# A gated Fourier mixer and state-space layer on one core: the scan over odd tokens only, products with W summed on VectorE, and turned x copied by VectorE

## The chip, the cores and the metric

One core of one Trainium2 chip runs the whole kernel. The metric is the device time of one execution in microseconds. A time is the median of several executions. Durations of single instructions come from one profiled execution, whose span runs from its first to its last instruction.

## What is computed

The input x has 2048 tokens of 1024 channels in bf16. Two branches work on the same x, and a gate per token mixes them (cut to what matters):

```
g = sigmoid((x * gate_w).sum(-1, keepdims=True))

# branch A: Fourier mixing over tokens and channels
X = rfft2(x);  X = X * (w_r + 1j * w_i);  a = irfft2(X)

# branch B: a diagonal complex recurrence over the tokens
Lam_bar = exp(exp(log_dt) * Lam)
Bu = einsum("bld,pd->blp", x, B_bar)
for t in range(L):
    h = Lam_bar * h + Bu[:, t, :]
b = 2.0 * einsum("blp,dp->bld", hseq, Cmat).real + x * Dskip

out = g * a + (1 - g) * b
```

The recurrence is the part with a serial nature: 2048 steps, 1024 complex states. Both Fourier transforms are done as matrix products in stages.

## The kernel before

The kernel writes its order by hand. The string `ORDER` holds one letter per step; each letter advances one generator (the table `acts`, from line 1167), and the letter v runs the next piece of the recurrence, in the order that `PIECES` gives. `SLOTS` says which of four PSUM slots (two banks each) the next PSUM tile takes. The order of the letters is thus the order of the instructions in each engine's queue: TensorE (PE in the profile), VectorE (DVE), ScalarE (ACT), GpSimd (POOL) and the queue of SyncE that issues most DMAs (SPq). An engine works through its own queue in order and waits where its next instruction's data or buffer is not ready.

The stages, with their letters:

- **Turning x** (x, T, U). x is loaded (`load_x`, L234), twelve of its sixteen column groups are transposed by TensorE into PSUM (`turn`, L913), and the other four by DMA. `turn_out` (L922) copies each of the sixteen groups into xQ, 1024 elements per partition: ScalarE does all of them. In xQ a chunk of 256 tokens lies in runs of eight tokens.
- **Forward Fourier transform** (f, F, E, S, A, 1). `fold` (L933) makes sums and differences on VectorE. `fd` (L420) is the transform over channels, `fd_out` (L446) copies its result out of PSUM, `s1` (L454) is the first part of the transform over tokens, `s1_out` (L466) copies that out. `FD_DVE` and `S1_DVE` name the copies that VectorE does (four and three of sixteen each); ScalarE does the others. `s1_store` (L478) writes to DRAM scratch. The gate is formed on the way (g, e).
- **Input product of branch B** (h, H). `unit_mm` (L391) is the product of x with B, 32 matmuls per step. It reads a whole chunk of xQ, and each turn step writes a sixteenth of every chunk, so all sixteen copies have to be done before the first h. `unit_out` (L402) casts the result to bf16 on ScalarE.
- **Recurrence** (v, `recur`, L334). There are eight chunks of 256 tokens; the first two are handled in two halves of four state blocks each, the others in one piece with eight blocks, so there are ten groups. States are rotated by tables (`make_tab`, L272, letter t) so that the step of the recurrence has a real factor, the radius r. A group is: two products with the tables (`cross`, `along`), a sum and a difference (`join_re`, `join_im`), the carry from the chunk before (`carry_in`), two scans (`scan`, L361; real and imaginary part, each over all tokens and blocks of the group), the carry to the next chunk (`carry_part`, `carry_sum`), two products back (`cross`, `along`), a sum and a difference (`out_re`, `out_im`). All of these run on VectorE.
- **Output product of branch B** (n, o). `c_half` (L707) and `c_part` (L722): sixteen matmuls of 512 columns for half of a tile of 128 tokens. They need the whole chunk's recurrence. Tiles 13 to 15 (`c_part`) end the kernel; tiles 14 and 15 need the last chunk.
- **Middle of the Fourier branch** (s, 3, 4, 5, 6, 7, 8). `s2` (L587) ends the transform over tokens, `s2_out` (L599) copies out, `times_w` (L612) multiplies with W on VectorE, `is1` (L621) is the first part of the inverse transform. A complex product has four real products; `times_w` forms the four and `is1` adds them up on TensorE: it takes four passes of eight matmuls for each of the eight groups, with four sign variants of its constant MT.
- **End of the Fourier branch** (i, I, l, p, z, P, Z, R, Q, D and others). `is2`, `spectral_mm`, `spectral_out`, and `spectral` (L820), sums and differences on VectorE; then the two branches are added and rows are stored (`close`, L856; `last_out`, L896; `last_store`, L903).

The lines of the scan in `recur`:

```
seg = u[:, ri, j:j + m].rearrange("p j t -> p (j t)")
nc.vector.tensor_tensor_scan(out=seg, data0=rz[...], data1=seg, initial=0.0, op0=ALU.mult, op1=ALU.add)
...
work.extend((lambda: scan(0, 0, n), lambda: scan(1, 0, n)))
```

Of the kernel before, what the change touches and what calls it, by code (L numbers as in the profile page):

```python
# [26 lines left out]
NCH = S // TC  # L27
NEARLY = 10
# [9 lines left out]
FD_DVE = (2, 4, 6, 7)  # L38
CAST_ACT = (5, 6, 7)
ANG_ACT = (4, 5, 6, 7)  # L40
CARRY_POOL = ()
S1_DVE = (1, 4, 5)
CLOSES = (0, 1, 2, 3, 10, 4, 5, 11, 12, 6, 7, 8, 9)
PIECES = (
# [6 lines left out]
)  # L51
SLOTS = (
    "0123012310231023102310230123012031201312031203101230132031231031201312303312013213021021013010320130",
    "1220123203201320130130120321023120320321021023120312301230231201302303120",
# [3 lines left out]
    "xxxTVUVVVaTfVVrrUGTGG|Tfaaa|UafFffftafftUftxFEfTETUFffU22xSEkSTSTArxAfffUAUFTTEUfffUFbxwxbxbbTUEFbfE",  # L58
    "1bT~SSUfuFSFAUUUU2bbtbfAF1AtbbtrFttrbEffE11EbEh11SStbttfttttAg1~HtfufhA~tetFSSFrKHrtu1EAvfAEhtttvttt",
    "SSFtbbvvvAtEttH1Avthtftv1cttwv1tcthccctttvtcch~HFtvftHvvhuHtvfStEettStAHhtAeKrvFctcvvFhEEHKtvwtcSvtS",  # L60
    "hvvKc1vcc1vAAKKvv1c1v1hcvswcsLMvvveHHekMYsssnNHvvhHnsvvvJWWMvs3vsvNvvsssssnvssnvvs4NMvv4Njvhv553vhvv",
    "YvyJJL46H4vv5WWvhh5vvvMM78Jj7HHmn3nHvv8M44m6MnN77WW5jv+Yy5vvv3M845+mNY8nMJJMyvvv+467hvHMh5vN7N34vHmh",
    "4J8m+6n3h8v77HmH+55v4n64JMvNnMYy5vW83n+v7N474vJ568vYmmNJ7dh7NWj+v58v5vyvvd88MhvHHm8+MJm6h+n378vv7Hh8",
    "J+d4Y4YX5vv5NnJH6XXv7ny7mNNm8+hn8hvqivvvvvJvqyHihYivvyiqhivqqiYvNImvni+qJJmHIIiini+HinvdIIH+vvIIIqIN",
    "IiiiNmI+vvIInvvImvyJqii%NJINIJYJYmhvvv+vvvlylzvhHmplpzZZH+mZZZhlZvhPPRR++zyRRRlQDQHzRZZmRHZ+ZRZvoOZD",
    "QvlpDzzPovOvQBvZZlpPYvZZvBZDZRDRRRvzQDoloOBzoQOopZOoPOBlzlZRoDDZZvBZZRpQvzCvYZZvZZBZZPRDoQoo9RQQ9yRR",
    "0RRyCooD099C9Y990DD0D0Y00",
# [6 lines left out]
HALF_PI = float(np.pi / 2)  # L74


def _host_consts():
# [15 lines left out]
    for u in range(4):  # L93
# [42 lines left out]
        MT=b16(np.concatenate([-np.cos(angM), -np.sin(angM), np.cos(angM), np.sin(angM)], axis=2)),  # L136
# [6 lines left out]
def kernel(  # L143
# [19 lines left out]
    out2 = out[0]  # L163
# [53 lines left out]
    nc.gpsimd.iota(tau_i, pattern=[[1, TC]], base=0, channel_multiplier=0)  # L217
# [5 lines left out]
    tab = tabp.tile([P, 4, 8, TC], BF16, name="tab")  # L223

    xn = [CT[i // 4][:, 2 * (i % 4):2 * (i % 4) + 2, :] for i in range(8)]
    x_v = x.rearrange("(p j) d -> p j d", j=16)
# [7 lines left out]
    def load_x():  # L234
        for i in range(8):
            if i >= NTURN // 2:
                g = i - NTURN // 2
                nc.sync.dma_start_transpose(out=xt[:, :, :, g].rearrange("p j d s -> p (j d) s"), in_=x_sg[g][:, NTURN * D:])
                yield
                continue  # L240
            for js in (slice(0, 1), slice(1, 2)) if i == 0 else (slice(0, 2),):
                nc.sync.dma_start(out=xn[i][:, js], in_=x_v[:, 2 * i + js.start:2 * i + js.stop, :])
                yield
# [19 lines left out]
    def cast(i):  # L263
        return nc.scalar.copy if i in CAST_ACT else nc.gpsimd.tensor_copy

    def radii():
        for jb in range(8):
            nc.gpsimd.tensor_copy(out=rz[:, jb, :], in_=r_sb[:, jb:jb + 1].to_broadcast([P, TC]))
            nc.gpsimd.memset(rz[:, jb, 0:1], 0.0)
            yield  # L270

    def make_tab(jp):  # L272
# [10 lines left out]
        sn_f = tmp.tile(sh, FP32, name="sn_f", tag="sn_f")  # L283
        cs_f = tmp.tile(sh, FP32, name="cs_f", tag="cs_f")
        yield from sincos(tmp, ang, sh, sn_f, cs_f, "rot")
        yield
        cast(2 * jp)(out=tab[:, 1, js, :], in_=sn_f)
        yield
        t1 = tmp.tile(sh, FP32, name="t1")
        t2 = tmp.tile(sh, FP32, name="t2")  # L290
        for j in range(2):
            nc.scalar.activation(out=t1[:, j], in_=sn_f[:, j], func=ACT.Copy, scale=ci[:, 2 * jp + j:2 * jp + j + 1])
        yield
        cast(2 * jp + 1)(out=tab[:, 0, js, :], in_=cs_f)
        yield
        for j in range(2):
            jb = 2 * jp + j
            nc.scalar.activation(out=t2[:, j], in_=cs_f[:, j], func=ACT.Copy, scale=ci[:, jb:jb + 1])
        yield
        for j in range(2):  # L300
            jb = 2 * jp + j
            nc.vector.scalar_tensor_tensor(out=tab[:, 2, jb, :], in0=cs_f[:, j], scalar=cr[:, jb:jb + 1], in1=t1[:, j],
                                           op0=ALU.mult, op1=ALU.subtract)
            yield
        for j in range(2):
            jb = 2 * jp + j
            nc.vector.scalar_tensor_tensor(out=tab[:, 3, jb, :], in0=sn_f[:, j], scalar=cr[:, jb:jb + 1], in1=t2[:, j],
                                           op0=ALU.mult, op1=ALU.add)
            yield

# [905 lines left out]
```

## Time and profile before

| | |
|---|---|
| median of three executions | 306.29 us (305.23 to 306.57) |
| span of the profiled execution | 303.6 us |
| mean granted TensorE clock | 0.999 |
| PE busy | 296.4 us, 98% of the span |
| DVE busy | 289.3 us, 95% |
| ACT busy | 188.5 us, 62% |
| POOL busy | 73.3 us, 24% |
| moved by DMA | 59.35 MB, 196 GB/s on average |

The span is 2.7 us shorter than the median time. Busy time is the union of an engine's instructions; the duration of one instruction contains its latency, so two neighbours in a queue overlap a little and the mean duration times the count is more than the busy time. This is strongest on TensorE, where a matmul of 256 columns shows 273 ns and the next one starts after about 114 ns. In lists of groups each line has the source line, the engine, the operation, output and inputs, shapes, count, then busy microseconds and the mean nanoseconds of one.

### The profile page before, as it was taken

The page shows a single profiled execution, that of the slowest core. Times are in us where ns is not written, and L with a number is a line of the kernel's source. Part 1 is how long each engine was busy: PE and PEld are TensorE (multiplying, and loading weights), DVE is VectorE, ACT ScalarE, POOL GpSimd, SP SyncE. Part 2 cuts the span into 40 slices and gives each one's busy share as a digit, 9 for nine tenths or more (in the row PEclk, how much of TensorE's full clock was granted, in tenths as well). Part 3 has the DMA queues.
Part 4 walks back from the last instruction along what each step waited for, and adds up shares of the span by engine and source line. Part 5 has one row for each costly group of instructions (what it writes and reads, how often), then busy time and mean ns, then how long its engine had stood idle before and what let it go on. Part 6 is the DMA issues. An engine that isn't in the chain of part 4 may idle for free. (4 is left out here: it accounts for less than half of the span.)

```text
span 303.6 us, 6402 instructions
## 1 busy us (share of the span) xinstructions
PE 296.4 (98%) x2568; PEld 197.4 (65%) x2592; DVE 289.3 (95%) x340; ACT 188.5 (62%) x255; POOL 73.3 (24%) x99
## 2 busy tenths in 40 slices
PE   8999999999999999999999999999999999999995
PEld 5664677878864685458553866669657986645543
DVE  2999999999999999999999999999899999999995
ACT  4999999896532383667665865529668774343400
POOL 2100420745893001110210220202011253252330
PEclk9999999999999999999999999999999999999999
DMA  6999999989999599895948798687758876978976
GB/s 208 341 201 194 253 193 310 162 142 154 268 214 241 160 259 219 181 250 189 212 96 258 163 223 225 139 294 147 242 174 185 165 88 135 160 132 143 165 153 181
DMA packets 74157, 59.35 MB, mean 196 GB/s; under 512 B 44904, under 2 KB 61680, under 8 KB 74128
## 3 DMA queue, kind: packets, MB, share of 16 engines
q1 hardware_dynamic: 66560, 49.82, 65.8%
q0 software_dynamic: 6912, 8.69, 23.0%
q10 hardware_dynamic: 656, 0.44, 0.5%
q8 instruction: 20, 0.33, 0.4%
q14 instruction: 9, 0.07, 0.1%
HBM read 27.46 MB, written 23.08 MB: 166 GB/s over the span
## 5 line engine op out<-in xcount | busy, mean ns | idle before, releaser
L398 PE MATMUL psu<-xQ,BT 128*128 128x256 bf16 x1024 | 116.5, 273 | 0.2 <-DVE X L449 0.2
L398 PEld LDWEIGHTS <-BT 128*128 128x128 bf16 x1024 | 99.0, 98 | 17.3 <-issue 4.6
L713 PE MATMUL ps_y<-CT,h 128*128 128x512 bf16 x397 | 92.5, 379 | 0.9
L363 DVE TENSOR_TENSOR_SCAN h<-rz,h 128x2048 bf16<-128x2048 f32 (+1 forms) x20 | 70.8, 3561 | 0.0
L713 PEld LDWEIGHTS <-h 128*128 128x128 bf16 x416 | 39.6, 98 | 46.3 <-issue 2.9
L785 POOL DMA_DIRECT2D y_scratch<-su x20 | 17.3, 902 | 135.7 <-ACT su L779 105.4
L408 ACT CAST h<-psu 128x1024 bf16<-128x1024 f32 x32 | 32.3, 1011 | 18.7 <-PE psu L398 13.1
L350 DVE TENSOR_TENSOR h<-h,tab 128x4096 bf16<-128x4096 bf16 (+1 forms) x20 | 37.1, 1859 | 0.1
L744 ACT ACTIVATE ye<-ps_y,omg 128x512 f32<-128x512 f32 x26 | 17.9, 689 | 26.3 <-PE ps_y L713 11.8
L347 DVE TENSOR_TENSOR xQ<-h,tab 128x4096 bf16<-128x4096 bf16 x12 | 27.4, 2284 | 1.0 <-ACT h L408 1.0
L603 ACT CAST X<-ps_s 128x1024 bf16<-128x1024 f32 x16 | 16.2, 1010 | 14.6 <-PE ps_s L594 11.2
L727 PE MATMUL ps_q<-CT,h 128*128 128x512 bf16 (+2 forms) x110 | 21.3, 348 | 0.2
L817 ACT ACTIVATE BT<-ps_id,gB 128x1024 bf16<-128x1024 f32 x14 | 15.3, 1114 | 9.9 <-PE ps_id L810 5.7
L671 ACT CAST ZT<-ps_is 128x1024 bf16<-128x1024 f32 x16 | 15.8, 1017 | 6.2 <-PE ps_is L661 6.2
L637 ACT CAST C<-ps_is 128x1024 bf16<-128x1024 f32 x16 | 15.7, 1011 | 5.1 <-DMA xQ<-in_A_x_dram 3.4
L851 POOL DMA_DIRECT2D BT<-y_scratch x10 | 13.1, 1452 | 19.7 <-DVE BT L846 13.3
L727 PEld LDWEIGHTS <-h 128*128 128x128 bf16 x112 | 10.3, 98 | 10.4 <-DVE h L378 0.5
L779 ACT ACTIVATE su<-xs,omg 128x512 f32<-128x512 bf16 x20 | 14.2, 723 | 4.1 <-DMA y_scratch<-su 2.2
L929 ACT COPY xQ<-pt 128x1024 bf16<-128x1024 bf16 x12 | 12.2, 1082 | 1.3 <-PE pt L919 1.3
L449 ACT CAST X<-ps_fd 128x1024 bf16<-128x1024 f32 x12 | 12.3, 1062 | 1.0 <-PE ps_fd L439 0.9
L617 DVE TENSOR_TENSOR UV<-X,Wb 128x2048 bf16<-128x2048 bf16 x8 | 9.6, 1220 | 0.6 <-ACT ye L744 0.6
L617 DVE TENSOR_TENSOR UV<-X,raw 128x2048 bf16<-128x2048 bf16 x8 | 9.8, 1223 | 0.2 <-ACT X L604 0.2
(200 smaller groups left out, 397.3 us busy)
## 6 DMA issues: line engine op xcount, KB each, us to landing
y_scratch<-ye SPq DMA_DIRECT2D x20, 256.0 KB, 4.6
y_scratch<-su POOLq DMA_DIRECT2D x20, 256.0 KB, 4.7
Bb<-turn_scratch SPq DMA_DIRECT2D x16, 256.0 KB, 5.2
turn_scratch<-C SPq DMA_DIRECT2D x16, 256.0 KB, 4.1
raw<-turn_scratch SPq DMA_DIRECT2D x8, 512.0 KB, 4.3
xs<-in_A_x_dram SPq DMA_DIRECT2D x13, 256.0 KB, 3.9
out_dram<-BT SPq DMA_DIRECT2D x11, 256.0 KB, 4.3
CT<-in_A_x_dram SPq DMA_DIRECT2D x5, 512.0 KB, 6.1
```

The lines of the kernel that those rows point to most:

```text
L347: nc.vector.tensor_mul(out=tmps["s"], in0=u[:, ::-1], in1=bc(i))
L350: nc.vector.tensor_mul(out=u, in0=u, in1=bc(i))
L363: nc.vector.tensor_tensor_scan(out=seg, data0=rz[:, js.start + j:js.start + j + m].rearrange("p j t -> p (j t)"), data1=seg, initial=0.0, ...
L398: nc.tensor.matmul(psu[:, j, :], lhsT=BT[4 * q + j][:, ri, d8, :], rhs=xQ[:, c, d8, :], start=(d8 == 0), stop=(d8 == 7))
L408: nc.scalar.copy(out=hs[c][:, ri, 4 * q:4 * q + 4].rearrange("p b (q j) -> p b q j", j=32), in_=psus.pop((c, q, ri)).rearrange("p b (j q) ...
L603: nc.scalar.copy(out=X2, in_=ps2s[g][b])
L617: nc.vector.tensor_mul(out=UV, in0=X2s.pop((g, b)).unsqueeze(1).to_broadcast([P, 2, 2, K]), in1=fft["Wb"][g // 2 % 2][:, :, at:at + 1, :]. ...
L671: nc.scalar.copy(out=ZT[:, 4 * kp:4 * kp + 4, :, 4 * G:4 * G + 4].rearrange("p (c r) n g -> p c r n g", c=2), in_=pszs.pop((G, kp)).rearra ...
L713: nc.tensor.matmul(psy, lhsT=hs[c][:, ri, jb, P * tq:P * (tq + 1)], rhs=CT[ri][:, jb, 512 * dh:512 * (dh + 1)], start=(i == 0), stop=(i == ...
L727: nc.tensor.matmul(psq, lhsT=hs[c][:, ri, jb, P * tq:P * (tq + 1)], rhs=CT[ri][:, jb, at:at + n], start=(i == 0), stop=(i == 15))
L744: nc.scalar.activation(out=ye, in_=psys[tb][:, K * hf:K * (hf + 1)], func=ACT.Copy, scale=omg[:, tb:tb + 1])
L785: nc.gpsimd.dma_start(out=y_dram[tb, hf], in_=xgs[tb, hf], accum_op=ALU.add)
```

## The change

The recurrence is split into even and odd tokens. hs, tab and rz get an axis e of two for the parity, with `TS` = 128 tokens each. Two steps of the recurrence are one step with the radius squared, from odd token to odd token. So after the join pieces, `fold_in` adds the even tokens' inputs to the odd tokens' inputs (the tables carry the needed factors), one scan of half the elements runs over the odd tokens with r squared, and the even tokens are filled in from the odd token before: ScalarE scales it (`next_`, one activation per state block), and VectorE adds (`fill_in`).

```
def fold_in():
    nc.vector.tensor_add(out=u[:, 1], in0=u[:, 1], in1=u[:, 0])
def scan():
    flat = lambda t, i: t[:, i, js].rearrange("p j t -> p (j t)") if n < 8 else t.rearrange("p r j t -> p (r j t)")
    for i in range(2 if n < 8 else 1):
        seg = flat(hs[c][:, 1], i)
        nc.vector.tensor_tensor_scan(out=seg, data0=flat(rz, i), data1=seg, initial=0.0, op0=ALU.mult, op1=ALU.add)
def next_(j):
    for i in range(j, j + 2):
        nc.scalar.activation(out=tmps["s"][:, 0, :, i, 1:TS], in_=u[:, 1, :, i, 0:TS - 1], func=ACT.Copy,
                             scale=r2_sb[:, js.start + i:js.start + i + 1])
def fill_in():
    nc.vector.tensor_add(out=u[:, 0], in0=u[:, 0], in1=tmps["s"][:, 0])
...
work.append(carry_in)
if c:
    work.append(carry_add)
work.extend((fold_in, scan))
if c + 1 < NCH:
    work.append(carry_part)
work.extend(partial(next_, j) for j in range(0, n, 2))
work.append(fill_in)
```

The sum of the carry's two parts moves from `carry_sum` into the next group's `carry_in`, which at chunk 0 is a memset. `make_tab` makes tables with the factors for odd tokens: the two forward tables are written by GpSimd (one copy and two scalings for a pair of blocks, in place of casts on GpSimd and ScalarE), and ScalarE scales the odd half by r.

`times_w` takes both halves b of a group in one product of 4096 elements and then subtracts and adds, so that `is1` has two passes in place of four:

```
nc.vector.tensor_mul(out=UV, in0=X2s.pop(g).unsqueeze(1).to_broadcast([P, 2, 2, 2, K]),
                     in1=W.unsqueeze(2).to_broadcast([P, 2, 2, 2, K]))
yield
nc.vector.tensor_sub(out=UV[:, 0, 0], in0=UV[:, 0, 0], in1=UV[:, 1, 1])
yield
nc.vector.tensor_add(out=UV[:, 0, 1], in0=UV[:, 0, 1], in1=UV[:, 1, 0])
```

The buffers of X2 and UV hold a whole group now, and there is one of each in place of two. MT loses one of its four variants.

x is loaded with its rows sorted so that a transposed group comes out with its tokens in runs of eight, by two DMAs of 64 partitions in place of one of 128; there are seven such steps. All sixteen copies of turned x go to VectorE, and the seven copies of `fd_out` and `s1_out` that VectorE did go to ScalarE:

```
-FD_DVE = (2, 4, 6, 7)
-S1_DVE = (1, 4, 5)
+FD_DVE = ()
+S1_DVE = ()
+TURN_DVE = tuple(range(16))
-                nc.sync.dma_start(out=xn[i][:, js], in_=x_v[:, 2 * i + js.start:2 * i + js.stop, :])
+                for g in range(2):
+                    nc.sync.dma_start(out=xn[i][64 * g:64 * (g + 1), js], in_=x_v[g, :, 2 * i + js.start:2 * i + js.stop, :])
...
+            (nc.vector.tensor_copy if j in TURN_DVE else nc.scalar.copy)(
+                out=x_gjq[:, :, :, :, j, :].rearrange("p c d g q -> p d g c q"), in_=src)
```

A tile of 128 tokens now is the even or the odd tokens of a chunk, so x, the gate and the output are read and written with rows two apart. ZT gets another layout to match. `PIECES`, `SLOTS` and `ORDER` are new from end to end: ORDER has 980 letters in place of 925 (55 more: 43 for the recurrence's pieces, 4 for the tables and 8 for the sums after the products with W).

More of the change, by code (lines that the diff above doesn't have):

```diff
@@ L1 @@
-import itertools
+from functools import partial
 from contextlib import ExitStack
@@ L27 @@
 NCH = S // TC
+TS = TC // 2
 NEARLY = 10
@@ L162 @@
     x = A_x[0]
-    out2 = out[0]
+    rows_of = lambda t: [t.rearrange("(c p e) d -> c e p d", p=P, e=2)[tb // 2, tb % 2] for tb in range(16)]
+    out_rows, x_rows = rows_of(out[0]), rows_of(x)
     hc = _host_consts()
@@ L327, in piece @@
         work[n] = None
-    def small_ops():
-        return nc.gpsimd if next(smalls_made) in CARRY_POOL else nc.vector
-    smalls_made = itertools.count()
+    units = {}
     def recur(c, js, home):
         n = js.stop - js.start
-        on_in, on_part, on_sum = (small_ops() for _ in range(3))
-        sh = [P, 2, n, TC]
-        u = hs[c][:, :, js, :]
+        sh = [P, 2, 2, n, TS]
+        u = hs[c][:, :, :, js, :]
+        tmps = units[c, js.start] = {}
         def bc(i):
-            return tab[:, i:i + 1, js, :].to_broadcast(sh)
-        tmps = {}
+            return tab[:, i, :, js].unsqueeze(2).to_broadcast(sh)
         def cross(i):
             tmps["s"] = home()
-            nc.vector.tensor_mul(out=tmps["s"], in0=u[:, ::-1], in1=bc(i))
+            nc.vector.tensor_mul(out=tmps["s"], in0=u[:, :, ::-1], in1=bc(i))
         def along(i):
@@ L1091, in turn_vectors @@
         nc.scalar.activation(out=r_sb, in_=are, func=ACT.Exp)
+        nc.scalar.activation(out=r2_sb, in_=are, func=ACT.Exp, scale=2.0)
+        nc.scalar.activation(out=rinv2, in_=are, func=ACT.Exp, scale=-2.0)
         yield
```

203 lines of the change are left out of this document (99 added, 104 removed), and 13 rows, old and new, of the table PIECES.

## The prediction

> **What bounds the kernel now.** I read the page's busy shares first, then a table of busy time by stretches, then the chain that ended last.
>
> ```profile
> PE 296.4 (98%) x2568; PEld 197.4 (65%) x2592; DVE 289.3 (95%) x340; ACT 188.5 (62%) x255; POOL 73.3 (24%) x99
> ```
> ```profile
> 0.00:6.00 6.00, 4.79 (x23) 2.45 (x24) 0.33 (x2) 2.02 (x2) 0.98 (x7) 1.00 0.65 206
> 10.00:35.00 25.00, 23.61 (x205) 15.11 (x210) 24.18 (x52) 25.00 (x32) 3.54 (x10) 1.00 1.14 230
> 60.00:286.50 226.50, 225.43 (x1980) 149.95 (x1998) 223.15 (x212) 134.56 (x180) 55.91 (x58) 1.00 0.86 187
> 286.50:300.50 14.00, 13.76 (x78) 7.07 (x79) 13.45 (x22) 0.92 (x1) 2.42 (x2) 1.00 0.86 198
> 300.50:303.60 3.10, 0.00 (x0) 0.00 (x0) 0.31 (x1) 0.00 (x0) 0.00 (x0) 0.93 0.27 84
> ```
> ```profile
> 285.42 1.15 DVE h L378
> 286.61 5.79 PE ps_q L727 x26
> 292.44 7.99 PE ps_q L727 x52
> 300.46 0.35 DVE raw L899
> ```
>
> After the length of each stretch, the columns are busy time of PE, weight loads, DVE, ACT and POOL. Two engines are full. From 60 to 286.5 us PE idles 1.07 us and DVE 3.35 us. From 10 to 35 us a third is full: ACT has no idle time at all. The chain shows how the two meet at the end: VectorE's last sum of the recurrence ends near 286.5, TensorE then multiplies two tiles for 13.8 us, and 3.1 us are left for the last sum and store.
>
> So the time moves only if both queues shorten, and each can be written as a sum. PE: 303.6 = 296.4 busy + 7.2 idle (1.2 at the start, 3.1 behind its last matmul, the rest mostly ahead of 35 us). DVE: 303.6 = 289.3 busy + 14.3 idle (5.7 ahead of 6 us, 2.8 at the end, the rest in small gaps).
>
> **Prices.** An instruction's duration contains latency that the next one hides:
>
> ```profile
> 261.14 0.68 DVE L838 TENSOR_TENSOR BT<-BT 128x1024 bf16<-128x1024 bf16 x1
> 261.74 4.42 DVE L363 TENSOR_TENSOR_SCAN h<-rz,h 128x2048 bf16<-128x2048 f32 x1
> 266.08 0.67 DVE L844 TENSOR_TENSOR BT<-BT 128x1024 bf16<-128x1024 bf16 x1
> ```
>
> The scan lasts 4.42 but the next starts after 4.34, the sum lasts 0.68 and the next starts after 0.60. So a place in VectorE's queue costs the duration less 0.08 us, and I use that for every row here:
>
> ```profile
> L363 DVE TENSOR_TENSOR_SCAN h<-rz,h 128x2048 bf16<-128x2048 f32 x12 | 52.7, 4416 | 0.0
> L363 DVE TENSOR_TENSOR_SCAN h<-rz,h 128x1024 bf16<-128x1024 f32 x8 | 18.1, 2278 | 0.0
> L347 DVE TENSOR_TENSOR xQ<-h,tab 128x4096 bf16<-128x4096 bf16 x12 | 27.4, 2284 | 1.0 <-ACT h L408 1.0
> L617 DVE TENSOR_TENSOR UV<-X,Wb 128x2048 bf16<-128x2048 bf16 x8 | 9.6, 1220 | 0.6 <-ACT ye L744 0.6
> L844 DVE TENSOR_TENSOR BT<-BT 128x1024 bf16<-128x1024 bf16 x7 | 4.8, 685 | 0.2
> L449 DVE CAST X<-ps_fd 128x1024 bf16<-128x1024 f32 x4 | 4.9, 1216 | 0.0
> L474 DVE CAST CT<-ps_s 128x1024 bf16<-128x1024 f32 x3 | 3.6, 1216 | 0.0
> L943 DVE TENSOR_TENSOR preT<-xQ 128x1024 bf16<-128x1024 bf16 x6 | 4.5, 747 | 0.4 <-ACT xQ L929 0.2 <-PE pt L919 0.2
> L302 DVE SCALAR_TENSOR_TENSOR tab<-cs_f,cr,t 128x256 bf16<-128x256 f32 x8 | 3.8, 501 | 0.1
> L1106 DVE TENSOR_SCALAR rot_kk<-ang 128x512 f32<-128x512 f32 x4 | 1.7, 418 | 0.0
> L629 PE MATMUL ps_is<-UV,raw 32*64 32x512 bf16 x256 | 8.6, 380 | 0.0
> L929 ACT COPY xQ<-pt 128x1024 bf16<-128x1024 bf16 x12 | 12.2, 1082 | 1.3 <-PE pt L919 1.3
> L925 ACT COPY xQ<-CT 128x1024 bf16<-128x1024 bf16 x4 | 4.0, 1193 | 0.0
> L279 ACT ACTIVATE ang<-tau_f,ang 128x256 f32<-128x256 f32 x4 | 2.0, 510 | 0.0
> L1149 ACT ACTIVATE xQ<-ident,vecF 128x128 bf16<-128x128 bf16 x8 | 2.8, 400 | 0.0
> ```
>
> **The change on VectorE.** *Scan.* Removed: 12 x 4.34 + 8 x 2.20 = 69.7. Six chunks now need one scan of 2048 elements each, 6 x 4.34 = 26.0. The four half groups need two scans of 512 elements each; the two scan rows give 2.14 us per 1024 elements, hence 1.21 and a place of 1.13, 8 x 1.13 = 9.0. Net -34.7.
>
> *Fold and fill.* Two sums per group over half of its elements: 2048 elements in six groups (1.14, by the L617 row of that size), 1024 in four (0.60). Twice 6.84 + 2.40 is +18.5. The carry pieces keep their number but for two small memsets, +0.2.
>
> *Products with W.* Removed 16 x 1.14 = 18.2. Added 8 products of 4096 elements at 2.20 (L347) = 17.6 and 16 sums of 1024 at 0.60 = 9.6. Net +9.0.
>
> *Copies.* Seven casts out of PSUM leave: 7 x 1.14 = -8.0. Sixteen copies of turned x come. No row shows VectorE copying bf16 out of PSUM. From above there is the f32 cast of the same size out of PSUM (1.14, L449). [...] The nearest row is L943: two bytes per element, 1024 elements, the same runs of eight in xQ. I take its 0.67 for the twelve from PSUM and 0.50, between L943 and L1106, for the four from SBUF: 8.0 + 2.0 = +10.0. The bounds are 16 x 0.34 = 5.4 and 16 x 1.14 = 18.2.
>
> [...]
>
> Together on DVE: -34.7 + 18.5 + 0.2 + 9.0 - 8.0 + 10.0 = -5.0; bounds -9.6 and +3.2.
>
> **On TensorE.** `is1` drops from 256 matmuls (8.6 us, eight small tiles sharing the array) to 128: -4.3. Everything else keeps its count, fillers too.
>
> **On ScalarE.** 64 activations of 254 bf16 elements come. The nearest row is L279 (256 elements, 0.51); L1149 with half the elements shows 0.40. With 0.5 each it is +32, with bounds 25.6 and 33. The turn copies go (-16.2), seven casts come (+7), the table work is about even. ACT ends near 211 of 300 us, so it is no bound in total.
>
> [...]
>
> **Where it meets the path.** *The scan's hand-over.* `fill_in` now waits for ScalarE: eight activations (4 us) for a whole group, four (2 us) for a half. Whatever follows `fill_in` in VectorE's queue waits with it, and TensorE behind that. I counted what the new ORDER puts on VectorE between a group's scan and its `fill_in`. For the last seven groups it is 5.1 to 13.9 us of other pieces, enough. For the first half of chunk 1 it is `carry_part` alone (0.2), so VectorE stands about 1.8 us. The other three early halves have 2.3 to 5.8 us with ScalarE's casts and table steps between; I allow 0.5 for them. Gaps: +2.3, bounds 0 and 8.
>
> *The first 35 us.* The first input product needs all sixteen copies.
>
> ```profile
> 25.51 4.03 ACT L925 COPY xQ<-CT 128x1024 bf16<-128x1024 bf16 x4
> ```
> ```profile
> 26.50 0.28 DVE L954 TENSOR_TENSOR preT<-sums 128x256 bf16<-128x256 bf16 x1
> 26.70 2.35 DVE L474 CAST CT<-ps_s 128x1024 bf16<-128x1024 f32 x2
> ```
> ```profile
> 30.33 3.65 PE L398 MATMUL psu<-xQ,BT 128*128 128x256 bf16 x32 [0.19 <-DVE X L449]
> 33.91 1.04 PE L462 MATMUL ps_s<-X,raw 64*128 64x512 bf16 x8
> 34.88 1.91 PE L1001 MATMUL zps_g<-xQ,gw 128*32 128x512 bf16 x32
> ```
>
> Now ScalarE ends the last copy at 29.5 and the product starts at 30.3. VectorE was past everything that ORDER put ahead of that copy at 26.7. In the new ORDER the same place has on VectorE the sixteen copies (+10.0), three casts fewer (-3.4), four more table steps (4 x 0.42, +1.7) and one more fold step (+0.6): 26.7 + 8.9 = 35.6. TensorE has three s1 units (a pair is 1.04, so 1.6) and the gate (1.9) more to do ahead of its first product, so it gets there at 30.1 + 3.5 = 33.6. It idles about 2 us (bounds 0 and 5).
>
> *x in halves.* Seven more DMA issues on SP's queue, which issues G, T2 and B's transposes behind them:
>
> ```profile
> 0.73 1.34 SPq L242 DMA_DIRECT2D CT<-in_A_x_dram  x3
> ```
>
> At 0.45 each that is 3 us spread over the first 25 us. The first turn needs two issues in place of one, 0.4 us later, while TensorE runs its warm-up matmuls. I cost it at nothing; without that cover it is at most 0.4 at the start.
>
> **The sum.** PE's queue: 303.6 - 4.3 + 2.0 = 301.3. DVE's queue: 303.6 - 5.0 + 2.3 = 300.9. The later one ends the span, 301.3. The median was 2.7 above the span, so the forecast is 304.0 us, 0.75% less. A measurement of this kernel can tell about 0.5% from no change, thus below 304.8 is faster and above 307.8 slower.
>
> **The rivals.**
>
> *Lean.* Both gaps vanish, since ScalarE, freed of the turn copies in a stretch where it has no idle time, serves TensorE's PSUM slots earlier. Then the span is 303.6 - 4.3 = 299.3, time 302.0. For it: the 25.00 of 25 in the second row of stretches. Against it: the 8.9 us more on VectorE ahead of the first product.
>
> *Copies at the full PSUM price (the other side).* If bf16 out of PSUM costs VectorE what f32 does, twelve copies cost 1.14 in place of 0.67, +5.6 in the first 35 us, where TensorE has nothing left to run ahead of its first product. Its queue is then 301.3 + 5.6 = 306.9, time 309.6, slower by 1.1%. It decides for slower from a price where 12 copies add 3.8: 0.99, which is a duration of 1.07 us. For it: the only VectorE casts out of PSUM in this trace last 1.216 us. Against it: with the new row order the copy reads and writes whole runs of eight two-byte elements, and an operation on such runs in SBUF (L943) takes 0.75.
>
> *Hand-over eats the gain.* If VectorE waits for ScalarE's activations in most groups, ten groups at 0.8 us in place of 2.3 in all: DVE's queue is 303.6 - 5.0 + 8 = 306.6, time 309.3; at half of that there is no change. For it: buffers of X2 and UV are single now, and ScalarE's queue is in order, so an activation can stand behind a cast that waits for TensorE. Against it: the count of pieces above.
>
> *The change doesn't do what it says* would be a scan that does not halve: 34.7 us more on VectorE. The two scan rows, nearly proportional to their elements, exclude that; no chance given.
>
> **How the numbers follow.** Forecast 0.45 (it reaches from 302.5 to 305.8 with its unknown terms): 0.27 faster, 0.16 same, 0.02 slower. Lean 0.26, all faster. Full PSUM price 0.17: 0.03 same, 0.14 slower. Hand-over 0.12: 0.05 same, 0.07 slower. Faster 0.53, same 0.24, slower 0.23. The range begins under the lean case, where VectorE's lower bound lets small idle times go as well, 299.0, and ends at the full price, 309.8. The forecast's own range is 302.5 to 305.8.
>
> **What would show it.** Right: scans of 2048 elements six times at 4.4 us and none else but eight of 512 near 1.2; `is1` near 4.3 us busy; turn copies on DVE near 0.75; PE busy near 292; the first input product near 36 us; VectorE idle at `fill_in` of chunk 1. Wrong: copies over 1.07 us, VectorE idle behind ScalarE in many groups, or the first product before 31 us (then lean holds).

## The result, and the profile after

The changed kernel takes 308.18 us (median; 306.38 to 310.77), the kernel before, measured beside it, 306.08 us. The ratio is 1.0069, with a 95% interval of 1.0048 to 1.0090: slower by 0.7%. The time lies inside the forecast range, but on the other side of no change: 304.0 was forecast. The profiled execution has a span of 305.2 us, 3.0 below the median. An execution's time is 1.8 us more than its own span; the rest is that the profiled one, at 307.0, is one of the shorter of the twenty.

The first line is the page's busy line of the kernel after; the rest are stretches in the same form as before (length; busy PE, weight loads, DVE, ACT, POOL; granted clock; DMA share; GB/s).

```profile
PE 292.3 (96%) x2442; PEld 195.2 (64%) x2464; DVE 289.1 (95%) x373; ACT 207.0 (68%) x309; POOL 70.8 (23%) x106
```
```profile
0.00:6.00 6.00, 4.79 (x26) 2.23 (x27) 0.93 (x3) 1.28 (x1) 0.99 (x7) 1.00 0.52 151
6.00:10.00 4.00, 2.24 (x39) 2.10 (x40) 3.86 (x18) 2.09 (x6) 0.48 (x2) 1.00 1.07 226
10.00:35.00 25.00, 20.78 (x183) 12.70 (x184) 22.73 (x57) 19.45 (x28) 8.09 (x18) 1.00 1.10 210
60.00:286.50 226.50, 224.70 (x1886) 151.02 (x1902) 221.68 (x232) 161.27 (x243) 47.94 (x63) 1.00 0.87 190
```

TensorE's idle time from 10 to 35 us grew from 1.39 to 4.22 us, and the stretch from 6 to 10 us now has 1.76 idle. TensorE's idle time over the whole span grew by 5.7 us (7.2 to 12.9); 4.4 of these lie in the first 35 us, the other 1.3 are spread over the rest (0.7 of them from 60 to 286.5 us), where some of it may be matmul records that are missing. So most of the loss is in the first 35 us, where the page's totals do not show it: PE's busy time fell by 4.1 us and the kernel got slower.

What TensorE and VectorE waited for after the change (engine, tile and line, releaser; us in total, times, longest):

```profile
PE pt L937 <- DMA CT<-in_A_x_dram: 4.9, 3, 1.9
```
```profile
DVE xQ L946 <- PE pt L937: 5.8, 4, 4.2
DVE h L375 <- ACT su L371: 1.2, 1, 1.2
DVE h L375 <- ACT xQ L371: 1.0, 1, 1.0
```

The first row is new: TensorE stands 4.9 us for x itself. VectorE's copies then stand for TensorE's turns. SP's queue after (start, time in issue, line, transfer, count) shows why:

```profile
0.72 2.57 SPq L246 DMA_DIRECT2D CT<-in_A_x_dram  x4
...
5.12 1.33 SPq L263 DMA_TRANSPOSE BT<-in_B_B_re_dram  x1
...
9.57 2.51 SPq L246 DMA_DIRECT2D CT<-in_A_x_dram  x4
12.12 1.31 SPq L263 DMA_TRANSPOSE BT<-in_B_B_re_dram  x1
13.48 1.23 SPq L246 DMA_DIRECT2D CT<-in_A_x_dram  x2
14.75 1.06 SPq L251 DMA_DIRECT2D raw<-c_T  x2
16.20 1.69 SPq L246 DMA_DIRECT2D CT<-in_A_x_dram  x2
18.27 8.04 SPq L241 DMA_TRANSPOSE CT<-in_A_x_dram  x1
```

And the same queue before:

```profile
11.11 0.58 SPq L242 DMA_DIRECT2D CT<-in_A_x_dram  x1
11.74 6.62 SPq L238 DMA_TRANSPOSE CT<-in_A_x_dram  x1
```

The last direct load of x left the queue at 11.7 before and 17.9 after, and the first transposed x starts 6.5 us later. Three transposes of B stand among the loads of x where one stood. And a half costs more to issue than a whole. Taken one by one, the seven whole loads last 0.33 to 0.72 us each in the queue before, 3.3 us together; the fourteen halves last 0.47 to 0.68 us each after, 8.0 us together. (A row of several also holds the gaps between them.) The first four halves, with nothing ahead of them, are no cheaper than the later ones: 2.57 us, 0.64 each, where the three whole loads of the forecast's row took 0.45 each. Why a half is dearer the traces do not show. The queue also stands ahead of each of the last two direct loads until an earlier transfer has landed, 1.1 us in all:

```profile
SPq L246 <- DMA CT<-in_A_x_dram: 1.1, 2, 0.7
```

The first input product of the kernel after:

```profile
38.01 3.66 PE L409 MATMUL psu<-xQ,BT 128*128 128x256 bf16 x32
```

It was at 30.33. The forecast had 36. Of the instructions themselves, the groups after show (total us, mean ns of one | idle ahead):

```profile
L367 DVE TENSOR_TENSOR_SCAN h<-rz,h 128x2048 bf16<-128x2048 f32 x6 | 26.5, 4416 | 0.0
L367 DVE TENSOR_TENSOR_SCAN h<-rz,h 128x512 bf16<-128x512 f32 x8 | 9.6, 1239 | 0.2
L946 DVE COPY xQ<-pt 128x1024 bf16<-128x1024 bf16 x12 | 8.1, 684 | 5.8 <-PE pt L937 5.8
L946 DVE COPY xQ<-CT 128x1024 bf16<-128x1024 bf16 x4 | 1.4, 420 | 0.4 <-DMA CT<-in_A_x_dram 0.4
L371 ACT ACTIVATE xQ<-h,r_sb 128x254 bf16<-128x254 bf16 x48 | 21.0, 521 | 0.0
L647 PE MATMUL ps_is<-UV,raw 32*64 32x512 bf16 x128 | 5.1, 386 | 0.0
```

Each of these is what the forecast said, or nearly (`is1` was to take 4.3). The durations were right and the result was not.

### The profile page after: what moved, and what is told of

Its sections match the earlier page's. It is cut to its first block, busy times and chain, and to the rows that moved or that the text cites. A ratio compares the mean times of both kernels' runs of the same rounds, so it can differ in the third digit from the quotient of the medians.

```text
span 305.2 us, 6250 instructions
## 1 busy us (share of the span) xinstructions
PE 292.3 (96%) x2442; PEld 195.2 (64%) x2464; DVE 289.1 (95%) x373; ACT 207.0 (68%) x309; POOL 70.8 (23%) x106
## 5 line engine op out<-in xcount | busy, mean ns | idle before, releaser
L342 DVE TENSOR_TENSOR h<-h,tab 128x4096 bf16<-128x4096 bf16 (+1 forms) x20 | 37.6, 1880 | 0.6 <-DMA raw<-c_MT 0.2
L367 DVE TENSOR_TENSOR_SCAN h<-rz,h 128x512 bf16<-128x512 f32 (+1 forms) x14 | 36.1, 2601 | 0.2
L339 DVE TENSOR_TENSOR xQ<-h,tab 128x4096 bf16<-128x4096 bf16 x12 | 27.4, 2281 | 0.0
L371 ACT ACTIVATE xQ<-h,r_sb 128x254 bf16<-128x254 bf16 x48 | 21.0, 521 | 0.0
L869 POOL DMA_DIRECT2D BT<-y_scratch x10 | 12.4, 1420 | 29.0 <-ACT xQ L1171 13.5
L460 ACT CAST X<-ps_fd 128x1024 bf16<-128x1024 f32 x16 | 16.2, 1020 | 3.9 <-PE ps_fd L454 3.1
L689 ACT CAST ZT<-ps_is 128x1024 bf16<-128x1024 f32 x16 | 17.2, 1149 | 0.0
L946 DVE COPY xQ<-pt 128x1024 bf16<-128x1024 bf16 x12 | 8.1, 684 | 5.8 <-PE pt L937 5.8
L299 POOL TENSOR_SCALAR tab<-sc,rinv 128x256 bf16<-128x256 f32 x8 | 10.3, 1296 | 10.3 <-ACT sc L294 10.3
```

The source lines that it names most:

```text
L339: nc.vector.tensor_mul(out=tmps["s"], in0=u[:, :, ::-1], in1=bc(i))
L342: nc.vector.tensor_mul(out=u, in0=u, in1=bc(i))
L367: nc.vector.tensor_tensor_scan(out=seg, data0=flat(rz, i), data1=seg, initial=0.0, op0=ALU.mult, op1=ALU.add)
L371: nc.scalar.activation(out=tmps["s"][:, 0, :, i, 1:TS], in_=u[:, 1, :, i, 0:TS - 1], func=ACT.Copy, scale=r2_sb[:, js.start + i:js.start + ...
L460: (nc.vector.tensor_copy if j in FD_DVE else nc.scalar.copy)(out=X1.rearrange("p r (m e c) -> p r m e c", e=2, c=2), in_=psf.pop(j).rearra ...
L689: nc.scalar.copy(out=fft["ZT"][:, kp, :, :, 2 * G:2 * G + 2], in_=pszs.pop((G, kp)).rearrange("p v (x n) -> p x n v", n=64))
```

## The experiments

The theory after the result: x comes late because it is loaded in halves, and the rest of the change is a small gain. Rivals: the new order of the queues makes x late; the products with W or the hand-over to ScalarE cost it; VectorE, whose busy time did not fall, is the bound. Ratios are to the kernel before, measured beside each kernel; line numbers in a row are those of its own kernel.

**Halves alone, in the kernel before.** Kernel before, with two transfers in place of one:

```
+                for g in range(2):
+                    nc.sync.dma_start(out=xn[i][64 * g:64 * (g + 1), js], in_=x_v[64 * g:64 * (g + 1), ...])
```

> The kernel before with each x step loaded by two DMAs of 64 partitions, its row order and all else kept. Theory (two issues per step delay the transposed parts of x): SyncE issues the first transposed part of x 2 to 4 us later than 11.7, the first product starts at 32 to 33 us in place of 30.3, the time rises by 1 to 2.5 us (ratio 1.003 to 1.008). Rival (issues are free beside the transfers): ratio 0.998 to 1.002.

Measured: 311.69 us, 1.0166 [1.0139, 1.0193]. Its SP queue, its first input product, and the stretch behind that product's start:

```profile
17.21 6.07 SPq L238 DMA_TRANSPOSE CT<-in_A_x_dram  x1
```
```profile
35.28 5.32 PE L399 MATMUL psu<-xQ,BT 128*128 128x256 bf16 x32 [2.02 <-ACT xQ L926]
```
```profile
36.00:39.40 3.40, 3.40 (x18) 2.36 (x17) 2.04 (x4) 3.40 (x7) 2.88 (x7) 0.50 0.93 232
```

The old order, with no transpose of B moved, has its first transposed x at 17.21 in place of 11.74 and the product 5 us later. The halves by themselves cost 1.7%, about 5.1 us, more than the expectation's 1 to 2.5 us. Not all of it is lateness: behind TensorE's wait of 2.02 us the granted clock is 0.50 for 3.4 us, in which TensorE loses up to 1.7 us. The kernel after shows no such stretch. Of the five executions, the only one with a mean clock of 1.00 took 310.88 us, still 4.4 above the kernel before.

**Undoing the halves, four ways that lost elsewhere.** First, one transfer with the halves as its outer dimension, in the kernel after:

```
+ in_=bass.AP(x.tensor, x.offset + D * (2 * i + js.start), [[16 * D, 2], [32 * D, 64], [D, m], [1, D]])
```

> The changed kernel with each x step loaded by one DMA whose source lists the rows in the sorted order (seven DMAs in place of fourteen), nothing else changed. Theory (x comes late because SyncE's queue has twice the issues ahead of the transposed parts of x): x's last direct issue ends near 13 us in place of 17.9, the first input product starts at 35 to 36 us in place of 38.0, TensorE's idle time ahead of 35 us falls by 2 to 3 us, and the time falls by 1.5 to 3 us, to a ratio with before of 0.997 to 1.002. Rival (the DMA engines, not the issues, set when x lands): the first product stays at 38 within 0.5 us and the ratio stays at 1.005 to 1.009. Rival (VectorE's full queue sets the time): the early idle time shrinks, but comes back later, and the ratio stays above 1.004.

Measured: 355.68 us, 1.1598 [1.1567, 1.1628]. Its first stretch:

```profile
0.00:6.00 6.00, 3.17 (x7) 0.88 (x7) 0.33 (x2) 1.28 (x1) 0.99 (x7) 1.00 0.06 21
```

A DMA share of 0.06 and 21 GB/s, against 0.52 and 151 after: with the outer dimension of 2 about one of the 16 engines was at work on average (0.06 x 16), where it was about eight after (0.52 x 16). TensorE stood 29.8 us for x in the first 50. The expectation missed.

Second, the halves of g=1 on ScalarE's queue, in place, and the same with x ahead of B's transposes:

```
-nc.sync.dma_start(out=xn[i][64 * g:...
+(nc.scalar if g else nc.sync).dma_start(out=xn[i][64 * g:...
```

> The changed kernel with the second half of each x step issued from ScalarE's queue, the first from SyncE's as it was. Theory (SyncE's issues delay x): SyncE reaches the first transposed part of x 3 to 5 us before 18.3, the first input product starts at 33 to 36 us in place of 38.0, TensorE's idle time ahead of 35 us falls from 7.2 to under 5 us, the time falls by 1.5 to 3.5 us, ratio 0.995 to 1.002. Rival (the DMA engines are full from 6 us on, so issues don't matter): first product within 0.7 us of 38, ratio 1.004 to 1.010.

> As e5, and x's issues and the mirror matrix JP ahead of the B transposes and of two parts of T2 (in the run with x first, TensorE stood 5.6 us for JP, which had been left behind the B transposes). Theory: the first product at 31 to 34 us, time 302 to 304.5 us, ratio 0.985 to 0.996, better than both kernels. Rival (DMA engines full): no better than the changed kernel, 1.004 to 1.012.

Measured: 316.58 us, 1.0317 [1.0267, 1.0367], and 316.12 us, 1.0301 [1.0249, 1.0352]. Both expectations missed. SP's queue did reach the first transposed x earlier (14.79 and 9.42 us in place of 18.27), but ScalarE's issues stand in its queue behind its own work (the last at 30.9 us in the first of the two); the first product is at 46.3 and 47.5. Third, all seven at the head of ScalarE's queue, and that with x first:

> The changed kernel with the seven second halves of x issued from ScalarE's queue at the kernel's start, so that none stands behind ScalarE's work as in the two runs before, where the last two were issued at 25 and 31 us. Theory (issues of x are the loss): the first transposed part is issued at 14 to 15 us in place of 18.3, the first product at 34 to 36 us, ratio 0.997 to 1.003. Rival (transfers, not issues, are the limit): first product within 0.7 us of 38, ratio 1.004 to 1.010.

> As e11, and SyncE's x issues and JP ahead of the B transposes and of two parts of T2. Theory: the first transposed part is issued near 9.4 us, the first product at 32 to 35 us, ratio 0.988 to 1.000, unless the B transposes, now last, hold the first product. Rival (transfers are the limit): ratio 1.004 to 1.012.

Measured: 315.26 us, 1.0299 [1.0253, 1.0346], and 311.05 us, 1.0164 [1.0119, 1.0209]. The seven issues at the head of the second kernel's queue:

```profile
2.94 9.39 ACTq L240 DMA_DIRECT2D CT<-in_A_x_dram  x7
```

Both missed again. Of the 9.39 us the seven issues themselves take 0.47 to 0.54 each; the rest is gaps, the longest 2.26 and 1.81 us. Each of these two ends 0.02 us after an earlier load of x has landed. So the second queue takes issues off SP's, but in this run it then stands for transfers to land, and ScalarE's first own work starts at 12.4 us. In both runs the granted clock is also 0.50 for a while (from 15.6 to 25.9 us in the first, from 8.3 to 11.7 in the second), so their loss is not that of the issues alone.

Fourth, one transfer per step with the rows as before, and copies that take every second token out of PSUM:

```
-    src = pts.pop(j).rearrange("p d (g c q) -> p d g c q", g=2, c=NCH)
+    src = pts.pop(j).rearrange("p d (c q g) -> p d g c q", g=2, c=NCH)
```

> The changed kernel with one DMA per x step and rows as before, the copies still on VectorE, now reading every second element from PSUM for the twelve. The copy should leave the fast rate: 1.2 us in place of 0.68, twelve times 0.5 = 6 us more on VectorE in the first 35 us. Theory (issues of x are the loss): what one DMA per step gives back, about 5 us, and what the slower copies take nearly cancel: first product 36 to 39 us, ratio 1.002 to 1.010. If the copies keep 0.68 us, the two DMAs were never needed: first product at 33 to 35 us, ratio 0.990 to 0.999.

Measured: 311.11 us, 1.0157 [1.0116, 1.0198], more than expected.

```profile
L945 DVE COPY xQ<-pt 128x1024 bf16<-128x1024 bf16 x12 | 14.4, 1220 | 5.3 <-PE pt L936 5.3
```

The copies take 1.220 us in place of 0.684, and the first product is at 42.7. x came in time (last direct load issued at 12.97), the copies did not. A second thing went wrong in the profiled execution: TensorE stood 3.6 us for the gate's weights ahead of 8.9 us and then had half its clock until 14.2, so the 1.57% is not the price of the copies alone.

**The order.** The kernel after, with x's places on SP's queue ahead of B's transposes:

> The changed kernel with only the order of SyncE's early issues changed: x's steps ahead of the B transposes and of two parts of T2, still two DMAs per step. Theory (what stands ahead of x in SyncE's queue delays it): about three transposes of 1.3 us leave the way, the first product comes 2 to 4 us earlier than 38.0, the time falls by 1 to 3 us. Rival (DMA engines are the limit): first product within 0.5 us of 38, ratio unchanged at 1.005 to 1.009.

Measured: 312.39 us, 1.0188 [1.0158, 1.0218]. Eight halves in a row took 5.86 us to issue; the first transposed x started at 15.33 in place of 18.27. But the constant JP came late, behind all of x:

```profile
PE ps_r L987 <- DMA JP_sb<-c_JP: 5.6, 1, 5.6
```

The granted clock is 0.50 from 33.8 to 40.6 us, around the end of that wait, and the first product is at 43.7. The expectation missed, and the run does not tell the two apart.

**The products with W.** The kernel after with the products and the four passes of before, then the kernel before with the sums and two passes (there 32 sums of 512 elements, in place of 16 of 1024):

```
-            nc.vector.tensor_sub(out=UV[:, 0, 0], in0=UV[:, 0, 0], in1=UV[:, 1, 1])
-            nc.vector.tensor_add(out=UV[:, 0, 1], in0=UV[:, 0, 1], in1=UV[:, 1, 0])
```

> The changed kernel with the products with W as before: sixteen products of 2048 elements and four passes of matmuls, no sums on VectorE. VectorE's busy time falls by about 10 us, TensorE's rises by 4. If VectorE's queue sets the time, it falls by 3 to 9 us (ratio 0.977 to 0.997). If TensorE's queue sets it, it rises by 3 to 4 us (ratio 1.017 to 1.020). If both are level, it stays within 1 us or rises by up to 3.

> The kernel before with the sums after the products with W on VectorE (32 sums of 512 elements behind their products) and two passes of matmuls in place of four. TensorE's busy time falls by about 4 us, VectorE's rises by 11 to 14. VectorE has 14 us of idle time in all, some 5 of them in the middle, so its queue should now decide: 5 to 9 us slower, ratio 1.016 to 1.030. If TensorE's queue alone set the time, 4 us faster, ratio 0.987.

Measured: without the sums 312.08 us, 1.0190 [1.0158, 1.0223]; the sums in the kernel before 317.81 us, 1.0350 [1.0300, 1.0401], more than expected. The first is 1.2% (3.7 us) above the kernel after, though its VectorE has 8 us less to do:

```profile
PE 295.9 (96%) x2570; PEld 197.3 (64%) x2592; DVE 281.2 (91%) x365; ACT 207.1 (67%) x309; POOL 71.9 (23%) x106
```

So in the kernel after TensorE's queue decides, and the sums are a gain. In the kernel before they are a loss, because there VectorE is full (busy for 95% of the span) and TensorE then waits for it:

```profile
PE ps_is L631 <- DVE UV L619: 8.3, 3, 2.9
```

Behind two of these waits (2.93 and 2.86 us) the granted clock is 0.50, from 136.4 to 143.2 and from 201.2 to 204.6 us, so a part of the 3.5% is the clock. That the halved scan is what makes room for the sums follows from the two runs together; the scan alone was not run.

**The hand-over to ScalarE.** The 64 activations are left out:

```
-            for i in range(j, j + 2):
-                nc.scalar.activation(out=tmps["s"][:, 0, :, i, 1:TS], ...
+            pass
```

> The changed kernel without the 64 activations that scale the odd tokens for the even ones (they are left out; fill_in adds what the products left in that buffer). It takes away the hand-over from VectorE to ScalarE and back, and 28 us of ScalarE. If the hand-over costs time, 2 us (its two waits on VectorE) to 4 us less than the changed kernel. If TensorE's queue sets the time and the early supply of x is the loss, within 0.7 us of the changed kernel.

Measured: 306.73 us, 1.0027 [1.0002, 1.0051], 0.42% (1.3 us) below the kernel after, between the two cases of the expectation. With both intervals that is 1.3 us, give or take 1. The two rows of 1.2 and 1.0 us above are where VectorE stands for it.

**The scan and W alone.** All of x's part undone (one transfer, copies on ScalarE, seven casts on VectorE), in the new order:

```
-TURN_DVE = tuple(range(16))
+TURN_DVE = ()
```

> The changed kernel with the whole x part undone: one DMA per x step with rows as before, turned x copied by ScalarE, the seven casts on VectorE again; the scan over odd tokens, the sums after W and the new order stay. So far the time followed the start of the first input product: 30.3 gave 306.3, 38.0 gave 308.2, 43.7 gave 312.4, 46.3 gave 316.6. Theory (the loss sits in x's early supply, the gain of 4 us on TensorE is there): the first product at 32 to 35 us, 303 to 306 us, ratio 0.990 to 0.999. Rival (the new order itself is worse, or ScalarE becomes the early bound with the copies back in an order not made for it): first product at 38 or later, ratio above 1.004.

Measured: 318.86 us, 1.0415 [1.0366, 1.0463], first product at 52.1. VectorE, ScalarE and TensorE wait for each other in turn, and the mean granted clock is 0.972. The expectation missed: a hand-written order fits one assignment of the copies, so this run cannot price x's part.

**How the halves cost.** It was still open whether the number of issues, the transfers of 64 rows or the order makes x late. First, the kernel after with steps 2 and 3 in one pair of transfers, and 4 and 5 in another:

```
+ if i in (2, 4):
+     nc.sync.dma_start(out=CT[i // 4][64 * g:64 * (g + 1), 2 * (i % 4):2 * (i % 4) + 4, :], in_=x_v[g, :, 2 * i:2 * i + 4, :])
```

> The kernel after, with the x of steps 2 and 3 in one pair of half transfers and that of steps 4 and 5 in another: ten direct issues in place of fourteen, the same bytes from the same 64 rows at a time. If the number of issues on SP's queue makes x late (about 0.64 us each in the profile after), the last direct x is issued about 2.5 us earlier, the first input product starts at about 35.5 us and the time is near 306. If it is the transfers themselves, or the three transposes of B among them, the first product stays at 37 to 38 us and the time at 307.5 to 308.5.

Measured: 310.29 us, 1.0176 [1.0159, 1.0194]. The last direct load left at 13.4 in place of 17.9, and still the first product is at 41.6. A step's turn now waits for a transfer that carries its neighbour's bytes too. The wait, and the granted clock in the stretches after it:

```profile
17.98 1.87 PE L943 MATMUL pt<-ident,CT 128*128 128x128 bf16 x16 [3.49 <-DMA CT<-in_A_x_dram]
```
```profile
16.00:19.00 3.00, 1.02 (x10) 1.05 (x11) 0.20 (x1) 0.70 (x1) 0.95 (x1) 0.62 1.21 249
19.00:22.00 3.00, 3.00 (x16) 1.85 (x15) 2.93 (x6) 0.00 (x0) 0.00 (x0) 0.50 0.92 188
22.00:25.00 3.00, 3.00 (x25) 2.18 (x23) 0.75 (x2) 1.21 (x2) 0.00 (x0) 0.74 1.03 287
```

TensorE stood for 3.49 us and then ran at half its clock (matmuls of a turn 1.87 us in place of 1.05). So the run has a second cost that the kernel after does not have, and says only that fewer issues alone do not help. The expectation missed.

Then the way round both: x in whole transfers as before, and the tokens parted by TensorE, for nothing. The turn multiplies by the identity with its columns put in the order even, then odd:

```
+    nc.gpsimd.tensor_copy(out=turned.rearrange("p (g s) -> p g s", g=2), in_=ident.rearrange("p (s g) -> p g s", g=2))
...
-            nc.tensor.transpose(out=pt[:, i, :], in_=xn[j // 2][...], identity=ident)
+            nc.tensor.transpose(out=pt[:, i, :], in_=xn[j // 2][...], identity=turned)
```

> The kernel after, with x in seven whole transfers with the rows as before, and even and odd tokens parted by TensorE: the turn multiplies by a matrix of ones whose columns are in the order even, then odd, so that the copies out of PSUM still read neighbours. Nothing else is changed, the order included. If two transfers per step are what costs (5.6 us in the kernel before with halves alone), the first input product starts at 33 to 35 us, the copies take about 0.68 us, and the time is 303 to 305, which is faster than before. If the new order is what makes x late, the first product stays behind 36 us and the time at 306.5 to 308.5.

> As the permuted turn, with x in whole transfers, and in the places of SP's queue in the order of the kernel before: x, the tables and the turn's constant as there, one transpose of B ahead of the last direct x in place of three. If x sets the time, the first input product starts at 30 to 33 us and the time is 301 to 304. If the three early transposes of B were wanted early, or the rest of the new order waits for something else, the first product moves by less than 1 us against the permuted turn alone, and the time is 305 or more.

Measured: 304.86 us, 0.9988 [0.9965, 1.0010], and 304.89 us, 0.9988 [0.9970, 1.0007]. Of the first, TensorE's stretches, SP's queue, the first product and the copies:

```profile
6.00:10.00 4.00, 3.46 (x52) 3.15 (x53) 3.86 (x17) 2.65 (x10) 0.48 (x2) 1.00 1.16 228
10.00:35.00 25.00, 22.99 (x210) 13.26 (x210) 24.73 (x63) 21.40 (x27) 8.30 (x18) 1.00 1.13 235
60.00:286.50 226.50, 226.08 (x1890) 149.59 (x1889) 221.81 (x229) 158.04 (x237) 46.87 (x59) 1.00 0.84 189
```
```profile
12.98 7.82 SPq L243 DMA_TRANSPOSE CT<-in_A_x_dram  x1
```
```profile
35.20 3.66 PE L410 MATMUL psu<-xQ,BT 128*128 128x256 bf16 x32
```
```profile
L947 DVE COPY xQ<-pt 128x1024 bf16<-128x1024 bf16 x12 | 7.9, 683 | 3.6 <-PE pt L938 3.6
```

The halves are undone, the identity of the turn is another matrix, the fast copies and the order stay, and 0.8% (2.5 us) comes back. The expectation held at the time (303 to 305) but called it faster than before, and that is not measurable. The first transposed x starts at 12.98 in place of 18.27: of the 6.5 us of lateness 5.3 are the halves and 1.2 the order. TensorE has no wait for x any more. Putting SP's old order back as well moves neither the product (35.6) nor the time: the rival of the order falls. From 60 us on TensorE has 0.4 us of idle time and VectorE 4.7, so there TensorE's queue is the full one.

**What is next late.** In the permuted turn VectorE has 0.27 us of idle time from 10 to 35 us. The permuted turn with steps 2, 5, 8, 11, or 9, 10, 11, copied by ScalarE:

```
+TURN_DVE = tuple(j for j in range(16) if j not in (2, 5, 8, 11))
```

> The permuted turn with four of its sixteen copies (steps 2, 5, 8 and 11) on ScalarE in place, the rest on VectorE. In the permuted turn VectorE has no gap from 7.8 to 36 us, and the first input product starts at 35.2 us. If VectorE's queue now sets that, 4 x 0.60 us leave it, the first product starts 2 us earlier and the time falls to about 303, measurably faster than before. If x or the order that was made for copies on VectorE sets it, ScalarE's copies (1.0 us each, behind its casts of X and A) come later than VectorE's did, the first product stays at 35 us or later, and the time is 305 to 307.

> As that with four copies, but the three last copies out of PSUM (steps 9, 10 and 11) on ScalarE, where VectorE has them at 24.8, 25.4 to 27.9 us. If VectorE's queue sets the start of the input products, 1.8 us leave it late in the stage and the first product starts at about 33.5 us, the time at 303 to 304. If not, the first product stays at 35 us or later, and the time is 305 or more.

Measured: 306.48 us, 1.0054 [1.0021, 1.0086], and 309.03 us, 1.0107 [1.0066, 1.0147]; first product at 37.2 and 40.5. Work left VectorE and the product came later; in both the second case of the expectation holds. In the second, VectorE stood here:

```profile
DVE preT L994 <- PE ps_r L988: 5.2, 1, 5.2
```

ScalarE's copies come behind its casts, and the folds and turns that follow them wait. The second also has half its clock from 9.2 to 12.6 and from 29.7 to 33.1 us. This shows that the order fits the copies where they are; it does not show that VectorE's load is no bound in another order.

## Why the prediction was wrong, step by step

**The step that failed: "x in halves ... I cost it at nothing".** It was worth 5.1 us in the kernel before (1.0166) and 2.5 us in the kernel after (1.0069 against 0.9988). Without it the kernel is not slower. In the prediction's terms, TensorE's idle time ahead of its first product was to grow by 2.0 us; in the first 35 us it grew by 4.4, and by 1.6 in the permuted turn. Three things were wrong in the step. First the price of an issue: seven more at 0.45 made 3 us. But a half is dearer than a whole, the fourteen take 4.7 us more than the seven, and the first transposed x starts 5.3 us later than with whole loads. It is not that the DMA engines are full: whole loads are issued in 0.43 to 0.58 us in the permuted turn from 8 to 13 us too, where the DMA share is 1.16 (6 to 10 us) and 1.13 (10 to 35). Second the cover: the warm-up matmuls hide the first pair alone, while each later pair stands ahead of a turn that TensorE wants, and it stands 4.9 us for them. Third, the transposes of B (1.3 to 1.5 us each) were named as standing behind x, when the new order puts three among it; that makes 1.2 us of the lateness, and it cost no time: with SP's old order put back in the permuted turn the time stayed. The row to look at was there: x's last load leaving at 11.7, with the product at 30.3. Issuing from another queue did not bring x either: in the first run with two queues SP's queue got ahead (14.79 us in place of 18.27), and x as a whole came no earlier (TensorE stood 10.2 us for it).

**What stays open.** Forecast were 2.3 us less, measured 2.1 more. The halves are 2.5 of these 4.4 us; without them the gain is 0.12%, where 0.75% was forecast, so about 1.9 us are missing still. Two findings bear on it, and neither was tried in the permuted turn. The hand-over costs 1.3 us of time, while the forecast put it on VectorE's queue alone, where by its own sum (300.9 against TensorE's 301.3) it would have cost nothing. And in four of the ten executions of the permuted turn the granted clock is 0.993 or 0.994, with times of 305.0 to 306.0 us, while none of the nineteen of the kernel before is under 0.998.

**The place price failed too, and hid.** "Duration less 0.08" gave -5.0 us on VectorE; its busy time fell by 0.2 (289.35 to 289.11, the sums of the two tables of stretches). The large groups changed as forecast, or nearly: scans 70.8 to 36.1, which is the -34.7; folds and fills +20.4; products with W 19.4 to 29.2; copies +9.5; casts -8.5. All durations together fell by less, and what went missing besides is the overlap. In the rows an instruction that takes its neighbour's result starts after its end:

```profile
48.68 1.22 DVE L339 TENSOR_TENSOR su<-h,tab 128x2048 bf16<-128x2048 bf16 x1
49.94 1.22 DVE L342 TENSOR_TENSOR h<-h,tab 128x2048 bf16<-128x2048 bf16 x1
51.19 0.69 DVE L345 TENSOR_TENSOR h<-h,su 128x1024 bf16<-128x1024 bf16 x1
51.80 0.68 DVE L348 TENSOR_TENSOR h<-su,h 128x1024 bf16<-128x1024 bf16 x1
```

L342 writes over what L339 reads and starts 0.04 after its end, L345 needs both and starts 0.03 after, while L348, with L345's result not among its operands, starts 0.08 before. Counted over all of VectorE's instructions, 288 of 339 neighbours overlapped before and 276 of 372 after. The sum of all durations fell by 1.8 us (313.2 to 311.4), the overlap by 1.3, where the place price had counted 33 more instructions with 0.08 us of overlap each. That the operands decide it is read from such rows and was not tried by itself. This error did not set the sign: without the sums VectorE had 8 us less to do and the time rose.

**What held.** *TensorE's -4.3* for `is1`, nearly: its group went from 8.6 to 5.1, PE's busy time by -4.1 (by -2.9 in the permuted turn; some matmul records are missing on all sides), and the time by 3.7 (the run without the sums). *The first product at about 36*: 35.2 once the halves are gone. *TensorE's sum* looks right by luck: 301.3 was forecast, and the profiled execution of the permuted turn has a span of 301.9. But that is the shortest of its ten, 3.0 under their median time where the forecast took 2.7; the median execution's span is 303.05, beside 303.7 for the kernel before. *The hand-over's +2.3* as a gap of VectorE: 2.2 in rows, 1.2 of it at chunk 1, where 1.8 was forecast, and 1.0 at a whole group, where none was. The rival in which it eats the gain in most groups is out. *The lean rival* is out: both gaps stayed. *Copies at the full PSUM price* is out for this kernel: 0.684 us each, beside the 0.75 of L943's row that the forecast took (a place of 0.60 in place of 0.67). But it is true of the strided copy, at 1.220: with whole transfers on both sides, 1.0157 against 0.9988 makes 5.2 us, where the rival had 5.6; with the wait and the clock told above that agreement is partly luck. So the two transfers bought the fast copies, at a price that took the gain. *The lower bound of 0.34* for a copy, L1106's 0.418 less 0.08, was an estimate that no row showed for a copy: the four out of SBUF met it (0.420 us each), the twelve out of PSUM did not (0.684). *ScalarE's activations* took 0.50 to 0.52 us, as the row of 0.51 had it.

## What to carry to other kernels

Price a split transfer on the queue that issues it: each part costs its own issue (here 0.47 to 0.68 us for a half), and what stands behind it in the queue comes later (the first transposed x by 5.3 us). Here the parts did not land ahead of their readers: TensorE stood 4.9 us for them. If a layout is wanted for a cheap copy (0.684 us in place of 1.220), look for an engine that already touches the data: here TensorE's turn parts the tokens with another constant. And before a sum of places on an engine counts overlap as saved, check who needs whose result (here 276 of 372 neighbours overlapped).

## What the runs showed of the hardware

- TensorE's granted clock was 0.50 for some us around or behind waits of TensorE. With a wait of 3.49 us that ended at 17.98 (steps paired) it was 0.50 from 16.7 to 23.6 us; in the kernel before with halves, with a wait of 2.02 us that ended at 35.28, from 36.0 to 39.4. In the kernel after, where the longest wait for x is 1.9 us, it stays at 1.00. With steps paired the lateness was paid twice: behind the wait sixteen transposes took 1.87 us in place of 1.05.
- On SP's queue a load of 64 partitions of x took 0.47 to 0.68 us to issue, one of 128 partitions 0.33 to 0.72 us (fourteen: 8.0 us, seven: 3.3 us).
- With direct transfers of x that have an outer dimension of 2 the kernel moved 21 GB/s in the first 6 us; with two transfers of 64 rows each, 151.
- A bf16 copy of 1024 elements out of PSUM on VectorE: 0.684 us with neighbours in the source, 1.220 with every second element; 0.420 out of SBUF.
- A turn against an identity with permuted columns cost TensorE no more here than against the identity (one transpose 0.219 us on average, 0.226 in the kernel after), and brought the columns in the order even, then odd.
